# The eleven-product form of x @ w_in from block three on

## The chip, the cores and the metric

The kernel runs on one core of a Trainium2 chip. The metric is the device time of one execution in microseconds (us); lower is better. A core has five engines with instruction queues of their own, each worked off in order: TensorE (PE, with PEld for its weight loads), VectorE (DVE), ScalarE (ACT), GpSimd (POOL) and SyncE (SP), which here issues transfers.

## The reference

Two steps follow each other. The first is a delta rule over 768 positions for 4 batches and 8 heads of 48; the second a two-layer network over the 3072 tokens that come out of it, with 384 model and 2048 inner columns, all in float32:

```python
for t in range(S):
    kt, vt, bt = (k_n[:, :, t], v[:, :, t], beta[:, :, t, None])
    y[:, :, t] = np.einsum('bhd,bhde->bhe', q[:, :, t], state)
    v_old = np.einsum('bhde,bhd->bhe', state, kt)
    state = state + bt[:, :, :, None] * np.einsum('bhd,bhe->bhde', kt, vt - v_old)
...
h = x @ w_in
relu6 = np.clip(h + 3.0, 0.0, 6.0)
g = h * relu6 / 6.0
return (g @ w_out).astype(np.float32)
```

k_n is k divided by its norm. x is y with the heads of a token side by side.

## The kernel before

The positions are worked off in 24 chunks t of 32 (128 rows: 4 batches of 32). In each chunk the rule becomes small matrix products. `prep` (L505) scales the keys on POOL (L510, kb), transposes keys and queries on TensorE (L524, pt) with a copy on ScalarE (L532, KQ), forms the chunk's score matrix (L547, sc) and masks it on VectorE (L558, L and LB; the mask mb is made on POOL in L486, and L498 makes bkb). The triangular systems of four chunks, a group, are solved together on VectorE: `inverse` (L746) does a transpose (L469), 30 steps of a multiplication (L759, pr) and a subtraction (L764, A) whose width grows from 30 columns to 240 and falls back, and a second transpose (L473, X). `chain` (L787) carries the state from chunk to chunk: ks (L806) reads it, VectorE makes R (L901, L909), pz (L827) multiplies by the inverse, ScalarE copies it (L927), su (L938) and L956 update the state; L843, L819, py (L827) and L863 make the output y, which TensorE transposes (L873, yt) and ScalarE copies into xT (L877).

Two chunks make a block of 256 tokens; there are 12 blocks. For each block, first the product with w_in runs on TensorE (the "up" part, into the tiles ph and g), then the product with w_out (the "down" part, into po).

The up part has two forms. In `up` (L982), per 128 of the 2048 columns, three products of 256 tokens are summed (L994, three pieces of 128 of the 384 model columns); ScalarE and VectorE then make g (L1001, L1004). In `up_by_eleven` (L1059) two 128-column pieces are done together. The 256 tokens by two pieces of the model columns, times these two pieces by two 128-column pieces of w_in, are computed by seven products of 128x128x128 in place of eight, with sums of weight tiles and of token tiles as factors; the third piece of the model columns is done directly by two products of 256 tokens, which count as four. So eleven stand for twelve. It starts with four products into one PSUM tile (`begin`), copied by ScalarE (L1080) and added up by POOL (L1030), while the tile collects the rest (`end`); VectorE adds the parts (L1093, L1097), ScalarE copies one (L1100) and forms the clipped factor in a buffer shared with the block's output tile o (L1104), and VectorE multiplies (L1107). The sums of weight tiles (S1, S2, S4, and a difference written over W21) are made once, on POOL (L1030 too), by `weight_sums` (L1032), whose steps are issued with the down part of block UF - 1, the one right before the first up part in this form. They use the tile sums_in, which serves other purposes early on. The sums of token tiles, T1x to T4x, are made on VectorE for each block (L1056, `token_sums`) when the second chunk of the block has arrived.

The down part of blocks 2 to 11 (L1154 for blocks 0 and 1) has seven quarter products for eight, L1218, with sums of g on VectorE (L1204) and of results on POOL or VectorE (L1228); each quarter product is done in two halves. Its results go out by transfers from SP (L1143).

The order of instructions is written out. Up to chunk 4 a string, ORDER, names each step. After it, a loop over chunks t from 5 issues 15 units per chunk; in each unit it issues the chain's and prep's steps by a fixed plan, then one unit of the network (`units`), then some steps of the inversion of the next group (`fill`). How many is set by `room`, from the load which the current mode is assumed to put on VectorE (USED and mode["mean"], both of which depend on whether a block is before UF), and from how much must be done by the end of the group. A down part has 14 units and an up part 16, so that a block takes 30 units, two chunks. The stretch of chunk 7 is the down part of block 2, that of chunk 8 the up part of block 3, and so on: chunk 12 has the up part of block 5.

A PSUM ring of four tiles (psM) is shared by ph, po, pt, pz, py and yt; a new tile takes the place of the one whose readers were issued first.

Of the kernel before, what the change touches and what calls it, by code (L numbers as in the profile page):

```python
# [44 lines left out]
def kernel(  # L45
# [969 lines left out]
                past.add(("up", blk))  # L1015
            yield

    UF = 5
    S1, S2, S4 = (sums_in[:, i] for i in range(3))

    def w_tiles(s, i):
# [10 lines left out]
    def weight_sums():  # L1032
        for j in range(0, NPR, 2):
            r = slice(j, j + 2)
            plus_minus(S1[:, r], W21[:, r], W22[:, r], ALU.add)
            yield
            plus_minus(S2[:, r], S1[:, r], W11[:, r], ALU.subtract)
            yield
            plus_minus(S4[:, r], W12[:, r], S2[:, r], ALU.subtract)
            yield  # L1040
            plus_minus(W21[:, r], W11[:, r], W21[:, r], ALU.subtract)
            yield
# [5 lines left out]
    def token_sums(blk):  # L1048
        if blk < UF or ("seam", blk * CB + 1) not in past:
            return  # L1050
        needs(("seam", blk * CB), ("seam", blk * CB + 1), ("up", blk - 1))
        B11, B12, B21, B22, _, _ = (
            x.rearrange("p (a b) -> p a b", b=16) for x in x_tiles(blk)
        )
        for out, a, b in ((T1x, B12, B11), (T2x, B22, T1x), (B12, B22, B12), (T4x, B21, T2x)):
            nc.vector.tensor_tensor(out=out, in0=a, in1=b, op=ALU.subtract)  # L1056
        past.add(("sums", blk))
# [228 lines left out]
    def mlp_units():  # L1286
# [10 lines left out]
        def downs(blk):  # L1297
            if blk >= FIRST:
                yield from down_by_seven(blk)
                return  # L1300
            for c in range(CB):
                for f in range(0, NFC, WF):
                    if c == 0:
                        needs(*(("read", ("ph", blk, f + i, None)) for i in range(2)))
                    down(blk, c, f)
                    yield

        for blk in range(1, N // CB):
            mode["of"] = "down"
            mode["mean"] = 0.72 if blk + 1 < UF else 0.4  # L1310
            sums = weight_sums() if blk == UF - 1 else iter(())
            for _ in downs(blk):
# [3 lines left out]
            if blk + 1 < N // CB:  # L1316
                mode["of"] = "eleven" if blk + 1 >= UF else "up"
                for n, _ in enumerate((up_by_eleven if blk + 1 >= UF else up)(blk + 1)):
                    if blk + 1 == FIRST and n >= HF:
# [231 lines left out]
```

## Time and profile before

| what | us |
|---|---|
| median of 3 runs (666.17 to 667.43) | 667.3 |
| the profiled execution | 665.93 |
| its span | 664.1 |
| TensorE busy in the span | 636.2 |
| VectorE busy | 487.1 |
| ScalarE busy | 272.1 |
| POOL busy | 203.5 |
| L994, products of 256 tokens, 384 records | 89.7 |
| L1066, products of 128 tokens with xT and w_in, 336 records | 67.4 |
| L1066, products of 256 tokens, 224 records | 57.6 |

Every float32 product shows as two records of a matmul and two of a weight load. "Busy" counts a stretch in which records overlap once. The chain of work that ended last follows each piece back to what released it; its version in order of time gives start, length and line of each piece. The busy times by window show, for any stretch of the span, how much each engine worked in it. In rows of the timeline, the brackets at the end give the idle time of the engine before that row and what ended it.

### The profile page before, as it was taken

Reading aid. Unit: us, or ns where it says so; the run is one execution under the profiler, and the core shown is the slowest. Engines: PE = TensorE matmul, PEld = TensorE weight load, DVE = VectorE, ACT = ScalarE, POOL = GpSimd, SP = SyncE. Lnnn points to the kernel's source line nnn. Section 1 sums busy time; section 2 is a strip of 40 time slices with the busy share of each in tenths; the row PEclk is TensorE's granted clock in tenths of the full one; section 3 lists DMA queues with packets and bytes.
Section 4 is the critical chain, followed back from the end, with each engine's and each line's share of the span. In section 5 each row is a group of like instructions: output and inputs, shape, how many; then the busy total and the mean of one; then the engine's idle time right before and its main releaser. Section 6 shows DMA issues by size and latency. Waiting matters only on the chain.

```text
span 664.1 us, 26330 instructions
## 1 busy us (share of the span) xinstructions
PE 636.2 (96%) x11544; PEld 568.1 (86%) x11544; DVE 487.1 (73%) x1146; ACT 272.1 (41%) x532; POOL 203.5 (31%) x320
## 2 busy tenths in 40 slices
PE   2769999999999999999999999999999999999997
PEld 1658987776789989989989999999999999999997
DVE  4899867898555697657979748989658998456353
ACT  5897679331233143142144244244244144153350
POOL 6531112003511320562254354064052241331430
PEclk9659999999999999999999999999999999999999
DMA  7897246212140030041030030020020020000000
GB/s 175 206 236 197 76 98 161 49 28 41 23 83 8 10 66 3 2 85 27 2 74 3 2 74 3 3 61 2 3 50 2 2 50 1 23 19 2 25 1 25
DMA packets 88499, 33.27 MB, mean 50 GB/s; under 512 B 80160, under 2 KB 83232, under 8 KB 88384
## 3 DMA queue, kind: packets, MB, share of 16 engines
q1 hardware_dynamic: 88128, 31.29, 20.9%
q8 instruction: 91, 1.49, 0.9%
q10 hardware_dynamic: 256, 0.30, 0.2%
q14 instruction: 24, 0.20, 0.1%
HBM read 26.84 MB, written 4.72 MB: 48 GB/s over the span
## 4 chain that ended last, share of the span: by engine, by line
PE 90%; DVE 3%; DMA 2%; SPq 2%; ACT 1%; issue 1%; POOL 0%; ACTq 0%; DVEq 0%; POOLq 0%
PE po L1218 28%; PE ph L1066 20%; PE ph L994 16%; PE po L1154 6%; PE ks L806 3%; PE pt L524 3%; PE su L938 3%; PE pz L827 3%; PE py L827 3%; PE sc L547 3%; PE yt L873 1%; DMA spare<-in_moe_w_in_dram 1%; PE pi L684 1%; DMA w_out<-in_moe_w_in_dram 1%; SPq L168 1%
## 5 line engine op out<-in xcount | busy, mean ns | idle before, releaser
L1066 PE MATMUL ph<-xT,w_in 128*128 128x128 f32 (+1 forms) x560 | 121.4, 321 | 0.7 <-ACT KQ L532 0.5
L994 PE MATMUL ph<-xT,w_in 128*128 128x256 f32 (+1 forms) x576 | 117.1, 353 | 0.9 <-ACT xT L877 0.6
L1218 PE MATMUL po<-w_out,g 128*128 128x192 f32 x640 | 110.6, 326 | 0.0
L994 PEld LDWEIGHTS ph<-xT,w_in 128*128 128x128 f32 x576 | 95.2, 194 | 13.9 <-ACT xT L877 1.0
L1218 PEld LDWEIGHTS po<-w_out,g 128*128 128x128 f32 x640 | 104.6, 190 | 0.5
L1066 PEld LDWEIGHTS ph<-xT,w_in 128*128 128x128 f32 x560 | 91.1, 191 | 5.9 <-ACT KQ L532 0.7
L1030 POOL TENSOR_TENSOR g<-g 128x256 f32<-128x256 f32 x112 | 67.9, 608 | 83.2 <-ACT g L1080 78.8
L1218 PE MATMUL po<-spare,g 128*128 128x192 f32 x480 | 86.7, 332 | 0.0
L1218 PEld LDWEIGHTS po<-spare,g 128*128 128x128 f32 x480 | 77.2, 190 | 1.8
L1001 ACT ACTIVATE g<-ph,halves 128x256 f32<-128x256 f32 (+1 forms) x96 | 41.0, 436 | 74.2 <-PE ph L994 74.2
L1228 POOL TENSOR_TENSOR o<-o,u 128x192 f32<-128x192 f32 x18 | 13.2, 731 | 175.8 <-ACT o L1225 97.2
L1080 ACT ACTIVATE g<-ph 128x512 f32<-128x512 f32 x56 | 33.4, 597 | 81.8 <-PE ph L1066 81.8
L1204 DVE TENSOR_TENSOR g<-g 128x512 f32<-128x512 f32 x80 | 55.5, 715 | 5.6 <-PE po L1218 5.6
L759 DVE TENSOR_TENSOR pr<-A 128x30 f32<-128x30 f32 (+9 forms) x150 | 57.5, 383 | 2.7
L764 DVE TENSOR_TENSOR A<-A,pr 128x30 f32<-128x30 f32 (+9 forms) x150 | 55.7, 371 | 3.7
L1004 DVE SCALAR_TENSOR_TENSOR g<-g,ph 128x256 f32<-128x256 f32 (+1 forms) x96 | 34.7, 371 | 29.4 <-ACT g L1001 29.0
L356 ACT ACTIVATE spare<-spare,places 128x768 uint16<-128x768 uint16 (+1 forms) x56 | 52.6, 944 | 2.8 <-DMA kf<-in_k_dram 1.7
L1093 DVE TENSOR_TENSOR g<-ph,g 128x256 f32<-128x256 f32 x56 | 23.5, 420 | 38.5 <-PE ph L1066 30.9
L1225 ACT ACTIVATE o<-po 128x192 f32<-128x192 f32 x40 | 13.2, 330 | 83.2 <-PE po L1218 79.6
L1154 PE MATMUL po<-w_out,g 128*128 128x384 f32 x128 | 45.2, 491 | 0.0
L1107 DVE SCALAR_TENSOR_TENSOR g<-o,g 128x512 f32<-128x512 f32 x56 | 40.7, 726 | 5.9 <-ACT o L1104 5.9
L1104 ACT ACTIVATE o<-g,halves 128x512 f32<-128x512 f32 x56 | 40.4, 722 | 8.7 <-DVE g L1107 5.7
(141 smaller groups left out, 989.1 us busy)
## 6 DMA issues: line engine op xcount, KB each, us to landing
kf<-in_k_dram SPq DMA_DIRECT2D x96, 48.0 KB, 2.4
qb<-in_q_dram SPq DMA_DIRECT2D x96, 48.0 KB, 2.8
vf<-in_v_dram SPq DMA_DIRECT2D x96, 48.0 KB, 2.2
out_dram<-o SPq DMA_DIRECT2D x92, 48.0 KB, 1.6
spare<-in_moe_w_in_dram SPq DMA_DIRECT2D x4, 768.0 KB, 5.9
w_out<-in_moe_w_in_dram SPq DMA_DIRECT2D x4, 768.0 KB, 6.0
w_out<-in_moe_w_out_dram SPq DMA_DIRECT2D x4, 768.0 KB, 6.9
spare<-in_moe_w_out_dram SPq DMA_DIRECT2D x4, 768.0 KB, 5.0
```

The lines of the kernel that those rows point to most:

```text
L356: nc.scalar.activation(out=z, in_=z if n else d.bitcast(I16)[:, :, :, 3], func=func, bias=places[:, n : n + 1], scale=scale,)
L759: nc.vector.tensor_tensor(out=pv, in0=A[:, j + 1 :, j].unsqueeze(2).to_broadcast([n, w, j]), in1=A[:, j, 0:j].unsqueeze(1).to_broadcast([n ...
L764: nc.vector.tensor_tensor(out=A[:, j + 1 :, 0:j], in0=A[:, j + 1 :, 0:j], in1=pv, op=ALU.subtract)
L994: nc.tensor.matmul(ph[:, cols], lhsT=w_in[:, s, f * 128 : (f + 1) * 128], rhs=xT[:, s, cols], start=(s == 0), stop=(s == NKT - 1),)
L1001: nc.scalar.activation(out=g, in_=ph, func=ACTF.Relu, bias=half, scale=1.0 / 6.0)
L1030: nc.gpsimd.tensor_tensor(out=out, in0=a, in1=b, op=op)
L1066: nc.tensor.matmul(ph[:, n], lhsT=w, rhs=x, start=start, stop=stop, skip_group_check=True)
L1104: nc.scalar.activation(out=r, in_=g, func=ACTF.Relu, bias=half, scale=1.0 / 6.0)
L1107: nc.vector.scalar_tensor_tensor(out=g, in0=r, scalar=1.0, in1=g, op0=ALU.min, op1=ALU.mult)
L1154: nc.tensor.matmul(pos[c][:], lhsT=gs[blk, f // 2][:, f % 2, c * P : (c + 1) * P], rhs=w_out[:, f, :], start=(f == 0), stop=(f == NFC - 1),)
L1204: nc.vector.tensor_tensor(out=A(f, *out, 4), in0=A(f, *a, 4), in1=A(f, *b, 4), op=op)
L1218: nc.tensor.matmul(ps[n][:], lhsT=A(f - f % 2, *a)[:, f % 2], rhs=b[:, f], start=(f == 0), stop=(f == HF - 1),)
```

## The change

The constant UF, the first block whose up part takes the eleven-product form, goes from 5 to 3:

```diff
-    UF = 5
+    UF = 3
```

It acts in five places:

```python
def token_sums(blk):
    if blk < UF or ("seam", blk * CB + 1) not in past:
        return
...
for blk in range(1, N // CB):
    mode["of"] = "down"
    mode["mean"] = 0.72 if blk + 1 < UF else 0.4
    sums = weight_sums() if blk == UF - 1 else iter(())
...
        mode["of"] = "eleven" if blk + 1 >= UF else "up"
        for n, _ in enumerate((up_by_eleven if blk + 1 >= UF else up)(blk + 1)):
```

So blocks 3 and 4 change from `up` to `up_by_eleven`, with the token sums that this needs; the sums of the weights are issued with the down part of block 2 and no longer with that of block 4; and the planner takes other values for the up parts of blocks 3 and 4 and for the down parts of blocks 2 and 3, which deals out the steps of the inversions of two groups differently. Blocks 5 to 11 keep their instructions, apart from the order in which the steps of the inversion fall around block 5.

## The prediction

> **What bounds the kernel now.** I read the page's busy shares and its chain first, then the chain in order of time for the borders of the stages, then busy times by stage, then VectorE's rows inside two stages. "Up n" and "down n" are the stretches in which TensorE works on the product with w_in and with w_out of block n.
>
> ```profile
> PE 636.2 (96%) x11544; PEld 568.1 (86%) x11544; DVE 487.1 (73%) x1146; ACT 272.1 (41%) x532; POOL 203.5 (31%) x320
> PE 90%; DVE 3%; DMA 2%; SPq 2%; ACT 1%; issue 1%; POOL 0%; ACTq 0%; DVEq 0%; POOLq 0%
> ```
>
> TensorE is busy 96% of the span and carries 90% of the chain, so fewer columns on TensorE are time won, as long as nothing makes it wait. The stages, in the order up 3, down 3, up 4, down 4, up 5, then up 6, down 6 and up 7:
>
> ```profile
> 230.38:257.21 26.83, 26.83 (x429) 23.03 (x428) 23.77 (x60) 9.56 (x20) 6.54 (x9) 1.00 0.23 46
> 257.21:281.52 24.31, 24.31 (x445) 23.24 (x444) 16.81 (x38) 5.09 (x12) 8.12 (x9) 1.00 0.01 3
> 281.52:308.35 26.83, 26.83 (x430) 23.03 (x428) 16.37 (x40) 9.56 (x20) 15.46 (x23) 1.00 0.36 69
> 308.35:332.66 24.31, 24.31 (x445) 23.24 (x445) 20.63 (x47) 4.77 (x11) 4.73 (x7) 1.00 0.01 2
> 332.66:359.10 26.44, 25.96 (x476) 23.43 (x476) 22.38 (x52) 12.82 (x26) 14.32 (x23) 1.00 0.24 48
> ...
> 383.41:409.40 25.99, 25.73 (x477) 23.56 (x476) 16.25 (x39) 12.93 (x26) 13.49 (x23) 1.00 0.24 49
> 409.40:433.71 24.31, 24.31 (x446) 23.24 (x445) 22.55 (x54) 5.90 (x13) 5.09 (x9) 1.00 0.01 3
> 433.71:459.47 25.76, 25.76 (x477) 23.41 (x476) 23.00 (x52) 12.92 (x26) 14.45 (x23) 1.00 0.20 41
> ```
>
> Columns: window, its length, busy us of PE, PEld, DVE, ACT and POOL, granted clock (1.00 throughout), DMA. Up 3 and up 4, in the old form, take 26.83 us each with no idle TensorE. Up 5, the first in the new form, takes 26.44; up 6 and up 7 take 25.99 and 25.76. The other thing to see is the third busy number: VectorE has 23.77 us of work in up 3, but 16.37 in up 4.
>
> **The change part by part.** *TensorE.* The chain in order of time has both forms undisturbed:
>
> ```profile
> 290.15 2.59 PE ph L994 x12
> ...
> 455.00 0.51 PE yt L873 x3
> ...
> 622.66 19.47 PE ph L1066 x144
> ```
>
> Twelve records of the old form take 2.59 us, 0.216 each; a block has 16 x 6 = 96 of them, 20.7 us. A block in the new form has 144 records, and up 11, with nothing in between, does them in 19.47. So a block is worth 1.25 us at best, and a clean up stage takes 26.83 - 1.25 = 25.58. For up 4 the bounds are up 6 and up 7, which gain 0.84 and 1.07. Its VectorE load in the new form is 16.37 - 6.15 (its L1004) + 8 x (0.42 + 0.29 + 0.73) for L1093, L1097 and L1107 = 21.7, between theirs. I take the middle: **-0.95**.
>
> *VectorE in up 3* is the doubtful step. The new form puts 8 x 1.44 = 11.5 us there for 6.25 removed. The triangular inversion of the next group (pairs of L759 and L764) lies there too: 34 of its operations are in up 3 now, against 21 in up 5 and in up 7. The planner that deals them out now counts blocks 3 and 4 as the new form and so sends some ahead; the order of the changed kernel's instructions keeps 27 in up 3. I compare that order with up 7, the same form, up to L863, because TensorE's transposes of y (L873) wait for L863 and the later records stand behind them in TensorE's queue. The first two rows are from up 5, the rest from up 7:
>
> ```profile
> 334.20 0.41 DVE L759 TENSOR_TENSOR pr<-A 128x234 f32<-128x234 f32 x1
> 334.64 0.81 DVE L764 TENSOR_TENSOR A<-A,pr 128x234 f32<-128x234 f32 x1
> ...
> 444.62 0.75 DVE L819 SCALAR_TENSOR_TENSOR y<-ks,parity,y 128x192 f32<-128x192 f32 x2 [0.39 <-ACT y L843]
> 448.43 0.42 DVE L1093 TENSOR_TENSOR g<-ph,g 128x256 f32<-128x256 f32 x1 [0.46 <-PE ph L1066]
> 454.30 0.55 DVE L863 TENSOR_TENSOR y<-y,py 128x384 f32<-128x384 f32 x1
> 454.99 0.52 PE L873 MATMUL yt<-ident,y 128*128 128x128 f32 x3
> ```
>
> Up 7 has 19 inversion operations ahead of L863; up 3 will have 22, and longer ones (still 210 columns at the end, where up 7 is down to 150). By undisturbed rows (0.32 at 150 columns, 0.37 at 210, 0.41 at 234 and over) that is 8.72 us for 7.05, with three more gaps of 0.03: 1.77 more. Two idle stretches of up 7 (the 0.39 and 0.46 in brackets) lie behind added operations and take up 0.85. So L863 comes 0.92 later than in up 7, where L873 already takes 0.18 longer than its usual 0.33. Up 3 becomes 25.76 + 0.92 = 26.68: **-0.15**. Bounds: 25.58 (-1.25) if idle time swallows all, and 28.8 (+1.95), worked out below; I stay by the count, whose model is the nearest stage.
>
> *Down 3.* In up 7 the last L1107 ends 4.24 us into down 7. In up 3 one more operation stands ahead of it (0.4): 4.6. Behind it the new order has eight operations (168 to 108 columns, 2.7), L901 0.6, L1204 0.6, two of 84 columns 0.55 and L909 0.55: R is ready 9.6 us into down 3, and TensorE asks for it at 9.9. Then come four short ones, the transpose L473 (1.97) and the second L1204, done at 13.1; the half product that reads it is due at 12.85. **+0.25**, bounds 0 and +0.7 (both points late by 0.4 more).
>
> *Up 5* is no longer the first. Its VectorE order becomes that of up 7 row for row, so 25.76 for 26.44. But 0.48 of the difference was TensorE waiting for the copy of keys and queries (L532), which stood on ScalarE behind L1104, which waited for the output transfer of the block before; its last piece took 2.79 us to land, against a median of 1.6. ScalarE waits for such a landing in up 5 and, without harm, in up 10: two of seven. I count 0.13 of it in up 5: **-0.55** (bounds 0 and -0.85), and 0.1 in up 3: **+0.1** (bounds 0 and 0.48).
>
> *What I cost at nothing.* The sixteen sums of weight tiles on POOL (L1030, 12.3 us) move from between 285 and 321 us to about 193 to 219. They pass kb, mb and bkb (L510, L486, L498): kb slips 1.5 us from 193.2, and TensorE reads it at 211.3. POOL is idle 10.0 and 10.7 us in down 2; without that, TensorE would wait for kb by what it slips. Their waits for TensorE concern tiles last read in up 2, and the L1228 behind them wait for later products anyway. The token sums (L1056, 2.1 us a block) fall where VectorE waits 2.39 us for POOL at the end of down 2; without this gap they cost up to 2.1 a block. ScalarE gains 3.3 us a stage on 9.56 and stays half idle; if late, its price is the 0.48 above. POOL gets 10.1 us of additions a block, as in up 7. SP's queue keeps its order; no transfer is added or moved.
>
> **Sum:** -0.95 - 0.15 + 0.25 - 0.55 + 0.1 = -1.3 us. The profiled execution took 665.93 us (span 664.1, 1.83 around it), so 664.6; the runs shown have a median of 667.3, 1.4 above the profiled one, and the same step gives **666.0**.
>
> **The rivals.** *All of it is won.* VectorE's extra work disappears in idle time: up 3 like up 7 (-1.07), down 3 unharmed, up 4 -0.95, up 5 -0.6: -2.6, 664.7. For it: up 7 has 2.76 us of idle VectorE, and TensorE's longest wait from up 5 to up 7 is 0.48. Against: 0.74 of that idle time lies ahead of the added operations.
>
> *Slower: VectorE becomes the bound in up 3.* Its work there is 23.77 - 6.25 - 7 x 0.43 + 11.5 = 26.0 us, over the clean 25.58. If it keeps the 2.76 idle of up 7, up 3 takes 28.8 (+1.95), down 3 starts late (+0.7), up 4 gives -0.84 and up 5 nothing: +1.8, 669.1. The whole turns to a loss once L863 comes 1.3 us later than the 0.92 counted. For it: inversion operations beside POOL take up to 0.81 instead of 0.41. Against: up 7 carries the same POOL work and is held up by 0.18.
>
> [...] I give this 0.03, within the slower case.
>
> *Nothing to see.* Late landings in up 3 and up 5 both (0.96, less the 0.23 counted): -0.6, 666.7.
>
> **How the numbers follow.** A measurement of this kernel can tell about 0.2%, 1.33 us, from no change. Forecast 0.36, nothing to see 0.12, all won 0.32, slower 0.20. The forecast lies next to the bound, so 0.08 of its chance falls beyond it, and 0.02 of the slower case stays within: faster 0.40, same 0.42, slower 0.18. The range runs from the case in which all is won to two thirds of the way into the slower one, 664.6 to 668.4; the forecast's own is 665.2 to 667.3.
>
> **What would show it.** Up 4 and up 5 near 25.9; up 3 near 26.7, with L873 waiting about 1 us for L863; in down 3 a second L1204 that comes just as it is wanted; up 6 onward unchanged. It is wrong if up 3 exceeds 27.5, if VectorE's rows beside POOL grow beyond those of up 7, or if the weight sums delay kb so that TensorE's transposes (L524) wait in down 2.

## The result, and the profile after

The changed kernel takes 671.4 us in the median of 6 runs (670.18 to 674.4), the kernel before 666.06 beside it (665.24 to 667.43): slower by a factor of 1.0082, with an interval of 1.0062 to 1.0102. The forecast was 666.0 in a range of 664.6 to 668.4.

The profiled execution took 672.11 us with a span of 670.4. The busy shares and the chain of its page:

```profile
PE 633.2 (94%) x11640; PEld 568.1 (85%) x11640; DVE 503.1 (75%) x1170; ACT 281.9 (42%) x548; POOL 224.6 (34%) x352
PE 85%; DMA 4%; DVE 4%; SPq 2%; ACT 2%; issue 2%; POOL 1%; ACTq 0%; DVEq 0%; POOLq 0%
```

TensorE has 3 us less work and yet the span is 6.3 us longer. Of these, 2.4 lie ahead of the change: down 2 begins at 208.5 us here and at 206.1 before; the experiments come back to that. The busy times by stage, in the order up 3, down 3, up 4, down 4, up 5, then up 6 and up 7, with the columns as before:

```profile
232.81:261.29 28.48, 25.73 (x476) 23.48 (x476) 25.11 (x57) 12.70 (x26) 14.42 (x23) 1.00 0.21 44
261.29:288.16 26.87, 24.38 (x446) 23.27 (x445) 22.34 (x51) 6.54 (x15) 9.73 (x12) 1.00 0.01 3
288.16:313.74 25.58, 25.58 (x477) 23.49 (x477) 16.80 (x40) 12.96 (x26) 13.56 (x23) 1.00 0.37 72
313.74:338.05 24.31, 24.31 (x445) 23.24 (x445) 22.41 (x54) 5.92 (x13) 5.65 (x8) 1.00 0.01 2
338.05:364.44 26.39, 26.02 (x476) 23.43 (x476) 22.52 (x52) 12.85 (x26) 14.42 (x23) 1.00 0.23 48
...
388.75:415.20 26.45, 25.92 (x478) 23.52 (x477) 16.56 (x39) 12.85 (x26) 13.57 (x23) 1.00 0.23 47
439.50:465.80 26.30, 25.96 (x478) 23.51 (x476) 23.05 (x52) 12.96 (x26) 14.47 (x23) 1.00 0.19 41
```

Against before: up 3 +1.65, down 3 +2.56, up 4 -1.25, up 5 -0.05, up 6 +0.46, up 7 +0.54. TensorE's waits from 200 to 664 us (total, times, longest):

```profile
PE ph L1066 <- issue: 2.5, 3, 2.0
PE pz L827 <- DVE X L473: 2.5, 1, 2.5
PE yt L873 <- DVE y L863: 0.8, 1, 0.8
PE ph L1066 <- ACT KQ L532: 0.7, 2, 0.4
```

Before, the same view has 0.5 for KQ and 0.3 of issue. Two losses are new and large. Rows of the timeline show where:

```profile
243.12 0.88 PE L827 MATMUL pz<-R,X 32*32 32x48 f32 x64
243.93 0.86 PE L547 MATMUL sc<-KQ 64*32 64x64 f32 x64
246.76 0.38 PE L1066 MATMUL ph<-xT,w_in 128*128 128x128 f32 x2 [1.97 <-issue]
...
270.12 0.61 DVE L909 SCALAR_TENSOR_TENSOR R<-ks,parity,R 128x384 f32<-128x384 f32 x1
...
271.66 1.93 DVE L473 STREAM_TRANSPOSE X<-A 128x1024 f32<-128x1024 f32 x1
...
273.74 0.88 PE L827 MATMUL pz<-R,X 32*32 32x48 f32 x64 [2.49 <-DVE X L473]
```

In down 3, R is ready at 270.73, but pz also multiplies by X, the inverse of the new group, and that comes from L473 at 273.59. Before, the same transpose ended 0.7 us ahead of its pz:

```profile
264.45 1.98 DVE L473 STREAM_TRANSPOSE X<-A 128x1024 f32<-128x1024 f32 x1
...
267.10 0.88 PE L827 MATMUL pz<-R,X 32*32 32x48 f32 x64
```

In up 3, TensorE stands for 1.97 us behind pz and sc, and the trace knows nothing that it waited for.

### The profile page after: what moved, and what is told of

The parts are those of the page before. It is cut to its first block, busy times and chain, and to the rows that moved or that the text cites. A ratio compares the mean times of both kernels' runs of the same rounds, so it can differ in the third digit from the quotient of the medians.

```text
span 670.4 us, 26640 instructions
## 1 busy us (share of the span) xinstructions
PE 633.2 (94%) x11640; PEld 568.1 (85%) x11640; DVE 503.1 (75%) x1170; ACT 281.9 (42%) x548; POOL 224.6 (34%) x352
## 4 chain that ended last, share of the span: by engine, by line
PE 85%; DMA 4%; DVE 4%; SPq 2%; ACT 2%; issue 2%; POOL 1%; ACTq 0%; DVEq 0%; POOLq 0%
PE po L1218 26%; PE ph L1066 24%; PE ph L994 10%; PE po L1154 6%; PE ks L806 3%; PE pz L827 3%; PE su L938 3%; PE py L827 3%; PE pt L524 3%; PE sc L547 2%; DMA w_out<-in_moe_w_in_dram 2%; PE yt L873 1%; ACT spare L356 1%; SPq L1143 1%; DMA kf<-in_k_dram 1%
## 5 line engine op out<-in xcount | busy, mean ns | idle before, releaser
L1066 PE MATMUL ph<-xT,w_in 128*128 128x128 f32 (+1 forms) x720 | 156.4, 321 | 2.9 <-issue 2.2
L1066 PEld LDWEIGHTS ph<-xT,w_in 128*128 128x128 f32 x720 | 117.1, 191 | 10.0 <-issue 2.2
L1030 POOL TENSOR_TENSOR g<-g 128x256 f32<-128x256 f32 (+1 forms) x144 | 88.1, 613 | 109.8 <-ACT g L1080 104.1
L1080 ACT ACTIVATE g<-ph 128x512 f32<-128x512 f32 x72 | 43.0, 598 | 107.0 <-PE ph L1066 107.0
L994 PE MATMUL ph<-xT,w_in 128*128 128x128 f32 (+1 forms) x384 | 73.1, 340 | 0.6 <-ACT xT L877 0.6
L994 PEld LDWEIGHTS ph<-xT,w_in 128*128 128x128 f32 x384 | 60.1, 197 | 8.6 <-ACT xT L877 1.0
L1093 DVE TENSOR_TENSOR g<-ph,g 128x256 f32<-128x256 f32 x72 | 30.1, 419 | 45.7 <-PE ph L1066 36.2
L759 DVE TENSOR_TENSOR pr<-A 128x30 f32<-128x30 f32 (+9 forms) x150 | 60.5, 403 | 3.4
L1107 DVE SCALAR_TENSOR_TENSOR g<-o,g 128x512 f32<-128x512 f32 x72 | 53.5, 743 | 9.0 <-ACT o L1104 8.9
L1104 ACT ACTIVATE o<-g,halves 128x512 f32<-128x512 f32 x72 | 52.1, 724 | 13.0 <-DVE g L1107 7.9
L1204 DVE TENSOR_TENSOR g<-g 128x512 f32<-128x512 f32 x80 | 55.3, 713 | 3.0 <-PE po L1218 2.9
L764 DVE TENSOR_TENSOR A<-A,pr 128x30 f32<-128x30 f32 (+9 forms) x150 | 55.1, 367 | 3.3
L1066 PE MATMUL ph<-beta_tok,sums_in 128*128 128x128 f32 x288 | 55.7, 275 | 0.3 <-issue 0.3
L510 POOL TENSOR_TENSOR kb<-kf,inv 128x384 f32<-128x384 f32 x24 | 21.2, 885 | 73.8 <-issue 42.6
```

Source lines behind the costliest of these rows:

```text
L759: nc.vector.tensor_tensor(out=pv, in0=A[:, j + 1 :, j].unsqueeze(2).to_broadcast([n, w, j]), in1=A[:, j, 0:j].unsqueeze(1).to_broadcast([n ...
L764: nc.vector.tensor_tensor(out=A[:, j + 1 :, 0:j], in0=A[:, j + 1 :, 0:j], in1=pv, op=ALU.subtract)
L994: nc.tensor.matmul(ph[:, cols], lhsT=w_in[:, s, f * 128 : (f + 1) * 128], rhs=xT[:, s, cols], start=(s == 0), stop=(s == NKT - 1),)
L1030: nc.gpsimd.tensor_tensor(out=out, in0=a, in1=b, op=op)
L1066: nc.tensor.matmul(ph[:, n], lhsT=w, rhs=x, start=start, stop=stop, skip_group_check=True)
L1080: nc.scalar.activation(out=gt, in_=ph[:], func=ACTF.Copy)
```

## The experiments

Sixteen runs were made, four of them of unaltered kernels. Three theories stood at the start. A: block 3 alone is to blame, by the late X and the standstill. B: the longer program is slower from its start. C: the new form loses in every block. "Down 2 to up 7" below is the time from the first record of the half products of block 2 to that of block 7, so it holds every stage whose instructions the change touches. The expectations call the same stretch "down 2 to down 8".

**The change again, the change without block 3, block 3 alone.** The first kernel is the changed one unaltered. The second:

```diff
-    UF = 3
+    UF = 4
```

In the third, block 3 takes the new form, block 4 the old one, though with the overwritten W21, and blocks 5 to 11 the new one:

```diff
+    NEW = {3} | set(range(5, N // CB))
-            mode["mean"] = 0.72 if blk + 1 < UF else 0.4
+            mode["mean"] = 0.4 if blk + 1 in NEW else 0.72
-                for n, _ in enumerate((up_by_eleven if blk + 1 >= UF else up)(blk + 1)):
+                for n, _ in enumerate((up_by_eleven if blk + 1 in NEW else up)(blk + 1)):
```

> The changed kernel once more, unaltered. Theory A (block 3 alone: the inverse X comes late in down 3, 2.5 us, and TensorE stands still in up 3 for 2.0 us without a visible cause): both waits are there again, and down 2 begins near 206 us, as before the change, since the 2.4 us that it began later in the first trace were chance; 669 to 671. Theory B (the longer program is slower from its start, ahead of every changed instruction): down 2 begins near 208.5 again; 671. Theory C (the new form loses in every block by its waits): as A in the sum, but with waits of 0.3 us and more in up 4 to up 7 each.

> The new form from block 4 on, so block 3 stays in the old form. Theory A: the dense stage of the inversion is left alone, up 4 gains about 1.2 us and up 5 some 0.3; 1 to 1.5 us faster than before, 665, and no wait for X in down 3. Theory B: the program is longer too, so down 2 begins 1 to 2 us later, and the sum is 0 to 1 us slower than before. Theory C: 1 us slower than before.

> Block 3 in the new form, block 4 in the old one, 5 to 11 as before. The sums of weights overwrite a tile that the old form of block 4 reads, so block 4 does the same work with other numbers. Theory A: the whole loss is here: up 3 at 28.5 us, down 3 at 26.9, up 4 at 26.8; 4 us slower than before if the start is alike. Theory B: 2 us slower by the start and about as much by the stages. Theory C: half of the loss, 2 us.

Measured 670.79 (ratio 1.0057, 1.004 to 1.0074), 668.51 (1.0039, 1.0016 to 1.0061) and 672.45 (1.0102, 1.0059 to 1.0144), against 666.86 before. C falls: block 4 gains, 1.25 us of up 4 in the changed kernel and 1.1 of the stages from down 3 to down 4 (50.1 for 51.1) in the second. In these three the late X (2.5 us) is there when block 3 is new and not otherwise, as A says. The second trace of the changed kernel reaches down 2 at 205.7 us, as early as the kernel before, which speaks against B. But the kernel without block 3, which should have gained, lost too, and had a standstill of its own, in the middle of the sc of up 5, where its code is that of before:

```profile
344.53 0.76 PE L547 MATMUL sc<-KQ 64*32 64x64 f32 x53
346.92 0.33 PE L547 MATMUL sc<-KQ 64*32 64x64 f32 x11 [1.63 <-issue]
```

So A is incomplete: a standstill can move to another block.

**An earlier inverse.** With the down part of block 2 (chunk 7), at least two steps of the next inversion are issued in each unit, and three in units 6 to 11, until three are left:

```diff
-                take(fill, int(due))
-                left, due = max(left - int(due), 0), due - int(due)
+                n = max(int(due), 2 + (6 <= u <= 11)) if t == 7 and left > 3 else int(due)
+                take(fill, n)
+                left, due = max(left - n, 0), max(due - n, 0.0)
```

> The changed kernel with the inversion of the third group dealt out faster in chunk 7: three steps per unit in units 6 to 11 and at least two in the others, so that about six of its steps leave up 3 and down 3 for down 2. Theory A: X is ready 2.3 us earlier, the wait for it in down 3 goes from 2.5 to below 0.5, and L863 in up 3 comes 1 us earlier; 2.5 to 3.5 us faster than the changed kernel, 668. Theories B and C: the waits move, and the sum changes by less than 1 us.

668.61 (1.0025, 1.0009 to 1.0042). Down 3 in its trace:

```profile
267.36 1.97 DVE L473 STREAM_TRANSPOSE X<-A 128x1024 f32<-128x1024 f32 x1
...
269.19 0.55 DVE L909 SCALAR_TENSOR_TENSOR R<-ks,parity,R 128x384 f32<-128x384 f32 x1
...
269.88 0.88 PE L827 MATMUL pz<-R,X 32*32 32x48 f32 x64 [0.33 <-DVE R L909]
```

X now ends 0.5 us ahead of pz; of 2.5 us of waiting, 0.3 for R is left. The median fell by 2.2 to 2.8. The standstill in up 3 stayed (1.8 us).

**What the standstills have in common.** The trace's DMA records offered a new theory, D. Queue 8 carries instructions:

```profile
q8 instruction: 91, 1.49, 0.9%
```

These are 91 packets of 16 KB. TensorE has 23,280 records in the changed kernel, one packet for 256 of them; kernels with 104 to 128 more small records of each kind fetch 92. I numbered TensorE's instructions in the order of the built program (four for a product, two for a transposition, one for a wait that stands alone) and laid the records beside them. These are the places behind 62 us, in the 18 traces of this study, where over 0.58 us pass from the start of one product to the start of the next (TensorE's idle time there is some 0.2 to 0.3 us less):

```
                                          stops   number modulo 256 of the next instruction
no named releaser (one names POOL)           37   194, 195 or 196, in all 37
a named releaser (X, R, y, KQ, sums ...)     40   many others, none of 194 to 196
```

And in each of the 37, TensorE went on 1.2 to 1.6 us (median 1.39) after a packet of queue 8 had landed. In up 3 of the changed kernel, pz and sc are just 256 instructions and lie between two such borders (9410 and 9666). They are done in 1.7 us. The next packet was asked for 0.97 us after they began, took 1.25, and the product behind it started 1.43 later. TensorE waits for its own instructions. The places without a stop agree. At none of the 1,489 borders behind 62 us did TensorE begin a stretch less than 1.20 us after its packet had landed. Behind the 377 packets that were asked for before the stretch ahead of them had begun there is none of these stops. Of 25 stretches with less than 3 us of work whose next packet was asked for over 0.4 us after they began, 24 end in one.

**Moving the borders from the front.** Small products that nobody reads were put ahead of everything: 52 (208 instructions) or 64 (256) in the changed kernel, 11 (44) in the kernel before, 52 in the one with the earlier inverse.

```diff
+        ring("pm", NPM, ("ahead",))
+        ahead = psM.tile([P, 512], FP32, name="ahead", tag=slot["pm"])
+        for _ in range(52):
+            nc.tensor.matmul(
+                ahead[0:32, 0:48], lhsT=ident[0:32, 0:32], rhs=ident[0:32, 0:48],
+                start=True, stop=True, skip_group_check=True, tile_position=(0, 0),
+            )
+        read(("ahead",))
         for word in ORDER.split():
```

> The changed kernel with 52 small fp32 products of ident ahead of everything on TensorE, which stands idle for its first 8 us; nobody reads their output. They put 208 instructions (104 weight loads, 104 products in the trace) ahead of TensorE's stream and change nothing else. Theory D: the standstill of 1.5 to 2.0 us in up 3 that the waits put down to 'issue' is TensorE waiting for its own instructions. Queue 8 of the DMA fetched them in 91 packets of 16 KB, which for the 23280 records of the page is one packet for every 256 instructions; in the changed kernel the 128 records of pz and the 128 of sc in up 3 fill exactly one such packet, are done in 1.6 us, and the next packet was only asked for 1.0 us after they began, took 1.25 us and could be used 1.4 us after that. Moved by 208 instructions the packets divide pz and sc among two of them: no 'issue' wait of over 0.8 us behind 200 us, up 3 takes 26.6 to 27.0 us where it took 28.48, and the median lies 1.2 to 2.2 us below the changed kernel's (some 669.0); the wait of pz for X stays at 2.5 us. Theory A (only the late X, and a standstill that comes from contention in block 3 itself): up 3 keeps its standstill at the first ph behind sc, and the time is 670 to 671.5.

> The same with 64 products, that is 256 instructions ahead. Theory D: the packets divide the work of up 3 just as they do in the changed kernel, so the standstill of 1.5 to 2.0 us comes back at the same place, the first ph behind sc in up 3, and the time is that of the changed kernel (670.5 to 671.5), within 0.5 us. A theory by which any work or delay ahead loosens the standstill expects it gone, as with 52 products.

> The kernel before with 11 such products ahead, 44 instructions: by the count of its stream pz and sc of the last chunk of up 3 then fill one packet of 256 instructions, as they do in the changed kernel. Theory D: a standstill of 1.5 to 2.2 us appears in up 3 at the first ph behind sc, though block 3 is the old one, and others between 60 and 175 us, where more short packets arise (1 to 2 us in sum): 668.5 to 671 us, 2 to 4 us above the kernel before. Theory A: the products lie in TensorE's idle start and nothing changes: 666.5 to 667.2.

> The changed kernel with the earlier inverse of the run before (two steps of the chain of the inverse taken in each of the first chunks, so that X is there in time) and the 52 products ahead: both losses taken away at once. Theory D: no wait for X and no 'issue' wait over 0.8 us behind 200 us; the stages from down 2 on sum to 457.0 to 457.8, against 458.0 before and 459.7 with the earlier inverse alone; a median of 665.5 to 667.0, no slower than the kernel before. Theory A: as with the earlier inverse alone, 668.3 to 669.

The times came out wrong under either theory: 677.87, 676.32, 673.48 and 675.12, against 667.11 before (ratios 1.0154, 1.0144, 1.0091 and 1.0113). The products themselves were slow, 82 ns a record, and put the first transposition off from 8.14 to 10.40 us (52) and 12.32 (64), and the borders moved through the first 60 us too; what each of these cost was not separated. The places bear D out in part. With 256 instructions more, the standstill in up 3 is back where it was, as D says:

```profile
246.59 0.88 PE L827 MATMUL pz<-R,X 32*32 32x48 f32 x64
247.41 0.86 PE L547 MATMUL sc<-KQ 64*32 64x64 f32 x64
249.81 0.38 PE L1066 MATMUL ph<-xT,w_in 128*128 128x128 f32 x2 [1.55 <-issue]
```

With 208 it is gone from there, as D says, and up 3 takes 26.96 us. But I had expected no standstill over 0.8 us at all: one stands in the middle of the next py, and another, of 1.5 us, in the sc of up 4:

```profile
247.69 0.86 PE L547 MATMUL sc<-KQ 64*32 64x64 f32 x64
248.47 0.49 PE L1066 MATMUL ph<-xT,w_in 128*128 128x128 f32 x2
...
254.34 0.78 PE L827 MATMUL py<-R,LB 32*32 32x48 f32 x52
256.25 0.36 PE L827 MATMUL py<-R,LB 32*32 32x48 f32 x12 [1.12 <-issue]
```

The third was a miss in its place. In the kernel before with 11 products, pz and sc of up 3 lie between two borders, but hardly anything happens:

```profile
244.71 2.75 PE L994 MATMUL ph<-xT,w_in 128*128 128x256 f32 x12
247.40 0.88 PE L827 MATMUL pz<-R,X 32*32 32x48 f32 x64
248.21 0.84 PE L547 MATMUL sc<-KQ 64*32 64x64 f32 x63
249.23 0.21 PE L547 MATMUL sc<-KQ 64*32 64x64 f32 x1 [0.18 <-issue]
```

The packet was asked for 0.70 us before the stretch began, not 0.97 after it. What runs before differs: here products of 256 tokens (0.22 us from one record to the next), in the new form products of 128 (0.11). Whether that is why the packet was asked for earlier was not shown: no run varied it alone. The kernel's standstills came at 72, 84, 97 and 102 us instead (0.5, 0.5, 1.4 and 1.5).

The fourth kernel, with the earlier inverse shown above and 52 products, has no wait for X, but a standstill of 1.6 us in the sc of up 4. Its stages from down 2 on took 458.6 us, where I had expected 457.0 to 457.8 and the kernel before takes 458.0.

From all ten traces I then read, for each place in a pair of stages, how long after the border the next packet is asked for. With that I counted which shifts should help and which should hurt.

**Moving the borders at 60 us.** The next products were written into a tile of the inverse ahead of its first product (L684), where TensorE waits about 1 us for VectorE anyway, so that the first 60 us stay as they are.

```diff
+            for n in range(0 if "ahead" in past else 8):
+                b, h = n % B, n // B % H
+                nc.tensor.matmul(
+                    ps[rows(b), h, :], lhsT=ident[rows(b), rows(b)], rhs=ident[rows(b), 0:HC],
+                    start=True, stop=True, skip_group_check=True,
+                    tile_position=(C * b, C * b),
+                )
+            past.add("ahead")
             for h in range(H):
```

> The kernel before with 8 such products at the same place, 32 instructions, some 0.1 us of work in a wait. Theory D: the packets now end behind short stretches: about 1.0 us each of issue at 71, 82 and 94 us, 0.5 at 97, 0.7 at 351 and 1.6 at 395 us: 3 to 5 us slower than the kernel before, 669.5 to 672, with no change of block 3 and nothing asked of VectorE. Against D (the loss comes from the work of the eleven-product form alone): 666.5 to 667.3.

> The form from block four on (UF = 4, block 3 old) with one such product at the same place, 4 instructions. Theory D: the standstill of 1.6 us at the sc of up 5 goes or falls under 0.3 us, because the packet now ends 4 instructions further on and the packet ahead of it is another; some 0.5 us is left at 421 us: 666.6 to 667.6, 1 to 2 us below the form from block four on alone (668.5), no slower than the kernel before. Against D: 668.0 to 669.0, one useless product of 0.01 us changes nothing.

> The changed kernel with 59 fp32 products of 32x32 by 32x16, read by nobody, written ahead of the first product of the inverse into the same tile, where TensorE waits 1.0 to 1.3 us for VectorE at 59 to 61 us. 236 instructions, nothing else changes. Theory D (TensorE takes its instructions in packets of 256; the next packet is asked for when one is begun, and can be used some 2.4 us after its transfer starts, so that a packet that is worked off in under 3.4 us leaves TensorE standing): counted through the traces so far, the short packets of up 3 (1.6 to 2.0 us of standstill) and of up 7 (0.6) go, and what is left behind 200 us is 0.4 to 0.6 us at 246 us; with up to 0.5 us for the products 668.0 to 669.5 in the median, 1.5 to 2.5 below the changed kernel; the 2.5 us of pz waiting for X in down 3 stay. Against D: at least 670.5, and up 3 still with 1.5 us of issue.

> The changed kernel with the earlier inverse and the 59 products at 60 us: late X and short packets both taken away, the likeliest version to beat the kernel before. Theory D with A: no wait of pz for X, issue behind 200 us at most 0.6 us; the stages from down 2 to down 8 sum to 252.5 to 253.5 us, against 253.4 before and 255.0 with the earlier inverse alone; 666.0 to 667.3 in the median. Against D: 668.3 to 669.

*Eight idle products slow the kernel before* to 671.8 (1.0075, 1.0057 to 1.0092), as much as the change did. Its waits of TensorE from 62 to 110 us, where before has 0.2 us of issue:

```profile
PE pt L524 <- issue: 1.2, 1, 1.2
PE pi L692 <- issue: 1.1, 1, 1.1
PE sc L547 <- issue: 1.1, 1, 1.1
PE pt L524 <- POOL sums_in L699: 0.8, 1, 0.8
PE pz L835 <- issue: 0.5, 1, 0.5
```

The two that I expected at 351 and 395 us did not come. *One idle product, four instructions, speeds up the kernel without block 3* from 668.51 to 666.43. The two were measured in different sessions, but their ratios to the kernel before, taken beside each, lie apart: 1.0039 (1.0016 to 1.0061) and 0.9995 (0.9982 to 1.0009). The sc of up 5 now runs through:

```profile
344.35 0.86 PE L547 MATMUL sc<-KQ 64*32 64x64 f32 x64
345.14 0.49 PE L1074 MATMUL ph<-xT,w_in 128*128 128x128 f32 x2
```

Of the 2.1 us, 1.5 are in the stages from down 2 to up 7 (252.8 for 254.3). D explains how one idle product can do that; A, B and C do not. *The other two* took 674.59 and 671.19, slower than expected, though their stages did what was counted: down 2 to up 7 in 254.3 us with X late, 252.5 with the earlier inverse, against 253.4 before. The loss lies ahead of that: behind the 59 products, which are themselves most of a packet (236 instructions), TensorE stood 1.7 and 1.6 us, until 66.7 and 63.7 us into the span. The first of the two also reached 60 us late, which leads to the last question.

**The first 60 us, and both causes at once.** Three unaltered kernels, for their traces, and the earlier inverse with the 59 products moved to the idle first 8 us, spread over four parts of the array:

```diff
+        for n in range(59):
+            b, c = n % B, 16 * (n // B)
+            nc.tensor.matmul(
+                ahead[rows(b), c : c + 16], lhsT=ident[rows(b), rows(b)], rhs=ident[rows(b), 0:16],
+                start=True, stop=True, skip_group_check=True, tile_position=(C * b, C * b),
+            )
```

> The kernel before, unaltered, for a second trace. If the first 60 us (to the first product of the inverse, which waits for loads) vary by chance, TensorE reaches that product at 60 to 63 us, as in the traces so far (60.3 in the first trace of before), and down 2 begins 145.5 us later; down 2 to down 8 take 253 to 254 us. If the changed kernel has a slower start of its own, this one is at 60.0 to 60.6.

> The changed kernel, unaltered: a third trace. Chance in the loads: the first product of the inverse at 60 to 63 us (so far 60.2 and 63.0), 145.5 us more to down 2; the stages from down 2 to down 8 take 255.5 to 257.5 us, with 1.5 to 2.0 us of issue in up 3 and 2.5 us for X. A slower start of its own: 62 to 63 us.

> The changed kernel, unaltered, a fourth trace; as the one before: by chance 60 to 63 us to the first product of the inverse; by a slower start of its own 62 to 63.

> The changed kernel with the earlier inverse and the 59 useless products ahead of everything, between 2 and 4 us, where TensorE stands idle for its first 8 us, so that they cost nothing themselves and make no short packet of their own (at 60 us they did: 2.0 us of standstill at 62 us). Theory D with A: the stages from down 2 to down 8 take 252.0 to 253.0 us as with the products at 60 us (252.5), and the standstill at 62 us is gone: 665.5 to 667.5 in the median, unless the shifted packets of the first 60 us, which no trace has shown in this place, cost 1 to 3 us.

| kernel | traces | first product of the inverse, us | down 2 to up 7, us |
|---|---|---|---|
| before | 2 | 60.3, 61.5 | 253.4, 253.7 |
| changed | 4 | 63.0, 60.2, 62.9, 60.0 | 257.3, 255.7, 256.4, 257.9 |
| from block four on | 1 | 60.9 | 254.3 |
| the same, 1 product at 60 us | 1 | 59.9 | 252.8 |
| block three alone | 1 | 62.7 | 258.9 |
| before, 8 products at 60 us | 1 | 61.3 | 253.0 |
| changed, 59 products at 60 us | 1 | 63.0 | 254.3 |
| earlier inverse | 1 | 60.8 | 255.0 |
| earlier inverse, 59 products at 60 us | 1 | 60.0 | 252.5 |
| earlier inverse, 59 products at the start | 1 | 62.3 | 253.0 |

Where products stand at 60 us, the first of them is counted.

B falls: the changed kernel starts like the other in two of four traces. Of the eight traces that have its first 60 us, four are there at 60.0 to 60.8 and four at 62.7 to 63.0. The start varies from run to run, and the waits between 30 and 45 us say with what. In the slow start of the third trace of the changed kernel (62.9) they hold these two, in the quick one of its fourth (60.0) no issue at all:

```profile
PE su L938 <- issue: 2.8, 1, 2.8
PE sc L547 <- issue: 0.7, 1, 0.7
```

The six traces of the two kernels have 0 to 0.5 us of issue there where the start is quick (60.0 to 60.3) and 3.1 to 3.6 where it is slow (61.5 to 63.0). The stages from down 2 on cost the changed kernel 3.3 us on average (256.8 against 253.55). The medians differ by 5.3 in the first measurement and by 3.9 in the second; the rest may be slow starts that came oftener, and six traces are too few to say.

With both causes taken away the kernel took 667.88, against 667.21 before (1.001, 0.9991 to 1.0029). Its waits from 200 us on:

```profile
PE ph L1066 <- issue: 0.8, 1, 0.8
PE ph L1066 <- ACT KQ L532: 0.5, 1, 0.5
PE ph L1066 <- DVE xT L1056: 0.5, 1, 0.5
PE pz L827 <- DVE R L909: 0.3, 1, 0.3
```

So no version was found that measurably beats the kernel before; two are level with it.

## Why the prediction was wrong

*The step that failed first is down 3 (+0.25).* Its walk along VectorE's rows was right: the last L1107 was to end 4.6 us into the stage and ended at 4.61, R was to be ready at 9.6 and was at 9.44, the second L1204 was to be done at 13.1 and was at 12.8. What failed is the list of who waits. I had L473 at its place in that walk, where it ends at about 12.4, and counted it only as something ahead of L1204; its own reader, pz, multiplies by X and was due at 9.9. X came at 12.3, and TensorE waited 2.49 us where I had 0.25. The earlier inverse removed just that. The margin that was spent, 0.7 us, stood in the trace of before.

*The second miss is not in any term: the standstill of 1.97 us in up 3* (1.5 to 2.4 in the four traces). I costed instructions by their durations and nothing for their number. A block in the new form has 96 more records on TensorE and shifts every later border between packets; in this kernel one border fell right behind the fastest stretch. What up 3 takes without it is best seen in the changed kernel with 59 products at 60 us, where a stop of only 0.60 is left:

```profile
251.99 0.38 PE L1074 MATMUL ph<-xT,sums_in 128*128 128x128 f32 x2 [0.60 <-issue]
...
259.44 0.55 DVE L871 TENSOR_TENSOR y<-y,py 128x384 f32<-128x384 f32 x1
...
260.14 0.52 PE L881 MATMUL yt<-ident,y 128*128 128x128 f32 x3
```

L871 and L881 are L863 and L873 there. Up 3 took 26.52, near the 26.68 that I had, and L863 came 0.8 later than in up 7 of the kernel before, where I had counted 0.92. But the transposes do not wait for it: the stop made TensorE as late as VectorE. The 0.78 that L873 waits in the changed kernel, which looks like the 1 us that I named as a sign, comes behind a standstill in which VectorE itself stood 1.43 us waiting for ph. So my count of VectorE's delay was about right, and what TensorE would have lost by it alone no run shows.

*Up 4 (-0.95)* gave -1.25, the clean bound. *Up 5 (-0.55)* gave -0.05 in the first trace: TensorE waited 0.4 for KQ in up 5 and again in up 6, where before had one such wait of 0.5 in up 5. But this wait comes and goes. In the four traces of the changed kernel up 5 takes 25.76 to 26.43 us, 26.2 on average, and in the two of the kernel before 26.45 and 26.89, so the forecast was about right there. Up 6, which lost 0.46 in the first trace, is level on average (25.9). *Late landing in up 3 (+0.1)*: none. Up 7, which I left unchanged, lost 0.54, and 0.5 to 0.8 in all four traces; a stop at one more border, at 452 us in the first trace (0.3), is part of it, and the rest I did not follow up. On average over the traces the stages thus cost +1.8 (up 3), +2.6 (down 3), -1.25 (up 4), -0.5 (up 5) and +0.6 (up 7): the 3.3 us from above, where I had -1.3.

*What I costed at nothing* held: the weight sums on POOL lengthened rows of VectorE in down 2 (beside them, L764 took 0.68 us at 30 and at 108 columns, where before has 0.21 and 0.27), which kept its 24.31 us, and no transposition waited for kb; the token sums held TensorE up only with the earlier inverse (0.5 us).

*The rivals.* The slower one had its cause in VectorE in up 3, with a price for down 3 behind it; VectorE was not the bound in up 3: of the 28.48 us, TensorE waited for it 0.78. That up 3 exceeded 27.5, which I had named as a sign of being wrong, came from the standstill. No run shows a ground for the 0.03 within the slower case: of the 17.4 us of L759, L764 and L1107 in up 3 of the changed kernel, 8.8 lie over rows of POOL, and up 3 took 28.48, of which 1.97 were the standstill. The gain that all sides expected is there: with both losses out of the way the stages of the earlier inverse take 252.5 and 253.0 us, 0.4 to 1.2 less than before, about the -1.3 of my sum at best, and too little to be seen in the medians.

## What to carry to other kernels

When an operation is moved later on a busy engine, list every reader of what each later operation in the queue writes, and compare its due time; the operation that I walked past had the earlier reader. And a product form with more, smaller products changes where TensorE's instruction packets end (here a block has 96 more records): where TensorE is the bound, look in the waits for "issue" on it behind bursts of small products, and try whether a few idle instructions, placed where TensorE waits anyway, move it. A change of some tenths of a per cent can't be judged without that: in the medians here, four instructions were worth 2 us, eight products 5.

## What the runs showed of the hardware

TensorE's instructions came in packets of 16 KB, 256 instructions: 91 packets for the 23,280 records of the changed kernel. At the stops, the next packet was asked for 0.5 to 2.9 us (median 1.1) after the stretch had begun; its transfer took 0.9 to 1.5, and 1.2 to 1.6 more passed until the first product. Of the 25 stretches with less than 3 us of work whose next packet was asked for over 0.4 us after they began, 24 left TensorE standing. Behind 377 packets that were asked for before the stretch began, by up to 3.7 us, there was none of these stops, even where the stretch took 1.6 to 2.3 us. The 37 stops, all but one without a named releaser, came at the numbers 194 to 196 modulo 256. The one in up 3 came back in each of the four traces of the changed kernel (1.5 to 2.4 us), was gone from there with 208 instructions put ahead and back with 256 (1.55 us). Between 30 and 45 us such waits came to 0 in one execution of the changed kernel and to 3.6 in another; why they vary is open.
